# Token order of a fused attention, expert and GLU kernel: one-hot products on TensorE in the place of eighteen 4-byte scatters

## Chip, cores and metric

One core of a Trainium2 chip. The metric is the device time in microseconds of one execution of the whole program.

## What is computed

Three layers in a row over 2304 tokens of 512 features: windowed attention, a layer in which each token goes to one of eight experts, and a gated layer. The expert layer and what follows it, cut to what matters:

```python
e_idx = np.argmax(x @ w_gate, axis=1)
for e in range(8):
    mask = e_idx == e
    h = np.maximum(x[mask] @ w1[e], 0.0)
    out[mask] = gate_w[mask, None] * eom[mask, e, None] * (h @ w2[e])
x = out
g = x @ w_gate2
y = (g * (1 / (1 + np.exp(-g))) * (x @ w_val) @ w_out)
```

`y` has the tokens in their old order.

## The kernel before

**Stages.** Attention runs over 18 blocks of 128 tokens until about 160 us. As it goes, every token gets its expert (`expf`) and its rank among that expert's tokens (`rankf`), and its row is scattered to the expert's area of a DRAM buffer `xs`. Then the experts are handled in the order of their sizes, p = 0 to 7, with up to 384, 384, 352, 336, 304, 272, 256 and 256 tokens (`CAPS`). For each, `emit_xT` (L917 to L919) transposes the gathered rows on TensorE into `tx`, ScalarE copies them out as `xh` and VectorE takes the remainder `xl`; 96 matmuls of L969 make `oh` from `xh`, `xl` and the weights `w`; ScalarE makes `hh` (L977) and VectorE `hl` (L981) for each of eight chunks; 96 matmuls of L995 make `oy` from `hh`, `hl`; `oy` is stored by columns into the DRAM buffer `ys`. Last comes the gated layer over nine units of 256 columns of `ys` (L1029 to L1053); each unit's two blocks of output rows go to their places in `out` by an indirect scatter on GpSimd (L1063), whose row numbers are `oid`.

**Weights.** Every weight is loaded in 256 KB pieces by SP into one of seven staging buffers (pool `stg`): `raw` for the experts (L302), `rawd` for the gated layer (L307, 64-bit numbers that VectorE and ScalarE narrow at L281 to L286). A piece is split into a high and a low part: ScalarE makes the high one (L326, L333), VectorE the low one for experts 0 to 2 and GpSimd for the others (L328, L334). `w_step` emits these two at a time between the chunks of L969 and of L995, so on ScalarE a conversion that waits for its load holds up the `hh` behind it. From expert 1 on a load's address holds the expert's number, which is known when the experts are sorted; the first pieces of the gated layer are mixed in from the second half of expert 2's weights on.

**The order of the tokens.** `expert_tables` (VectorE, some forty small operations) sorts the experts and finds where each one's columns begin. `token_order` (L794 to L825) then finds for every token its column in `ys`: `at` (start of the expert plus rank) and `far` (for tokens beyond an expert's capacity), added to `col`, one number for each of 128 partitions and 18 blocks. Its table `scr` is a staging buffer. Eighteen indirect DMAs on GpSimd (L819) write the tokens' numbers (`toki`), 128 of 4 bytes in each, to the places `col` of a DRAM table `order`. `load_order` (L829 to L832), called at p = 2, reads the table back into `oid` as [128, 18, 1]. `overflow_tables` makes tables for tokens beyond capacity and their count `nov`, which every engine reads (L1079).

**What sets the order of the work.** Attention's order is written out by hand. Behind it a scheduler orders each engine's instructions by their data and its own estimate of times; on an engine they then run strictly in that order, and so do the DMAs of one queue.

Of the kernel before, what the change touches and what calls it, by code (L numbers as in the profile page):

```python
# [7 lines left out]
F32 = mybir.dt.float32  # L8
F32R = mybir.dt.float32r
BF16 = mybir.dt.bfloat16  # L10
I32 = mybir.dt.int32
# [15 lines left out]
def attn_moe_glu_kernel(ctx, tc, q, k, v, w_gate, w_ogate, w1, w2, w2_gate, w2_val, w2_out, out, caps=CAPS):  # L27
# [32 lines left out]
    xs = dram.tile([E * NT + 1, RW], F32, name="xs")  # L60

    ys = dram.tile([DM, NT + cap], F32, name="ys")
    order = dram.tile([NT, 1], I32, name="order")
    assert NT % 256 == 0 and caps[0] + sum(caps[1:]) >= NT and min(caps) >= 256 and CP <= 512
    NOV = (NT - min(caps) + 127) // 128
    ov_pad = dram.tile([128, NOV], I32, name="ov_pad")
# [18 lines left out]
    rankf = const.tile([128, NBLK, 1], F32, name="rankf")  # L85
    capt = const.tile([128, 1, E], F32, name="capt")
    ktab = const.tile([128, E], F32, name="ktab")
    toki = const.tile([128, NBLK], I32, name="toki")

    with ExitStack():  # L90

# [57 lines left out]
        bias = ac.tile([128, H, 128], F32, name="bias")  # L149
        tmp, tmp2 = (p_p.tile([128, 4, 128], F32, tag="p", name="tmp") for _ in range(2))  # L150
        dist, mf, mu, mt = (tmp[:, i, :] for i in range(4))
        c64, dist_i = tmp2[:, 0, :], tmp2[:, 1, :].bitcast(I32)
        mge = ac.tile([128, 128], U8, name="mge")
        m_start = ac.tile([128, 128], U8, name="m_start")
        m_mid = ac.tile([128, 128], U8, name="m_mid")
# [36 lines left out]
        it2 = ac.tile([128, 32], I32, name="it2")  # L192
        nc.gpsimd.iota(it2[:, 0:NBLK], pattern=[[128, NBLK]], base=0, channel_multiplier=1)
        nc.vector.tensor_copy(tokid, it2[:, 0:NBLK])
        nc.gpsimd.tensor_copy(toki, it2[:, 0:NBLK])
        for p in range(E):
            nc.gpsimd.memset(capt[:, 0, p:p + 1], float(caps[p]))
            nc.gpsimd.memset(ktab[:, p:p + 1], float(E - 1 - p + (1 << 15) * (p == 0)))
# [549 lines left out]
        def tb(name, shape, dt=F32):  # L748
            return tb_p.tile([128] + shape, dt, tag=name, name=name)
# [43 lines left out]

        def token_order():  # L794

            more, behind = tb("more", [1, E]), tb("behind", [1, E])
            TT(out=more, in0=cnt, in1=cape, op=ALU.subtract)
            TS(out=more, in0=more, scalar1=0.0, scalar2=None, op0=ALU.max)
            nc.vector.tensor_copy(behind, more)
            for e in range(1, E):  # L800
                TT(out=behind[:, :, e:e + 1], in0=behind[:, :, e - 1:e], in1=behind[:, :, e:e + 1], op=ALU.add)
            TT(out=behind, in0=behind, in1=more, op=ALU.subtract)
            TT(out=behind, in0=behind, in1=cape, op=ALU.subtract)
            TT(out=behind, in0=behind, in1=offe, op=ALU.subtract)
            TT(out=behind, in0=behind, in1=total.to_broadcast([128, 1, E]), op=ALU.add)
            own, pick = scratch()
            at, lim, far = (tb(nm, [NBLK, 1]) for nm in ("at", "lim18", "far"))
            full = [128, NBLK, E]
            TT(out=own, in0=iota8.unsqueeze(1).to_broadcast(full), in1=expf.to_broadcast(full), op=ALU.is_equal)
            for src, dst in ((offe, at), (cape, lim), (behind, far)):  # L810
                TT(out=pick, in0=own, in1=src.to_broadcast(full), op=ALU.mult)
                RED(out=dst, in_=pick, axis=AX, op=ALU.add)
            TT(out=at, in0=at, in1=rankf, op=ALU.add)
            TT(out=lim, in0=rankf, in1=lim, op=ALU.is_ge)
            TT(out=far, in0=far, in1=lim, op=ALU.mult)
            col = tb("col", [NBLK, 1], I32)
            TT(out=col, in0=at, in1=far, op=ALU.add)
            for j in range(NBLK):
                r = nc.gpsimd.indirect_dma_start(  # L819
                    out=order[:, :], out_offset=bass.IndirectOffsetOnAxis(ap=col[:, j, :], axis=0),  # L820
                    in_=toki[:, j:j + 1], in_offset=None,
                ).ins
                tc.declare_no_dep(r, group="order", reason="the columns of the tokens differ")
                tc.add_to_no_dep_group("order", r)
                ordered.append(r)  # L825

        ordered = []

        def load_order():  # L829
            r = nc.gpsimd.dma_start(out=oid, in_=order.rearrange("(j p) o -> p j o", p=128)).ins  # L830
            for x in ordered:
                tc.add_manual_dep(r, x.name, DATA, reason="all tokens have columns")  # L832

# [119 lines left out]
        for p in range(E):  # L955
            n = caps[p]
            xh, xl = xe.pop(p)
            if p == 0:
                token_order()
                overflow_tables()  # L960
            if p == 2:
                load_order()
            hh, hl = (grid(t, KF, n) for t in pair_tile(ht_p, "h", HW))
            for m in range(KF):
                o = ps_m.tile([128, cap], F32, tag="m", name="oh")
                i = 0
                for a, b in PASSES:
                    for kk in range(KD):
                        pace[0] = nc.tensor.matmul(  # L969
                            out=o[:, 0:n],  # L970
                            lhsT=wt["w1", p, m // 4, kk][:, a, (m % 4) * 128:(m % 4) * 128 + 128],
                            rhs=(xh, xl)[b][:, kk, :],
                            start=(i == 0),
                            stop=(i == 3 * KD - 1),
                        )
                        i += 1
                r = nc.scalar.activation(out=hh[:, m, :], in_=o[:, 0:n], func=AF.Relu).ins  # L977
                if p == 0 and m > 0:
                    with tc.issue_after(r):
                        off_reg[m] = nc.scalar.value_load(reg[0:1, 1, m:m + 1], min_val=0, max_val=NT)  # L980
                STT(out=hl[:, m, :], in0=o[:, 0:n], scalar=0.0, in1=hh[:, m, :], op0=ALU.max, op1=ALU.subtract)  # L981
                w_step(2)
                if m % 4 == 3:
                    freed[0] += 2
            if p + 1 < E:
                emit_xT(p + 1)
                load_x(p + 2)
            else:

                split_unit(0)  # L990
            o = [ps_m.tile([128, cap], F32, tag="m", name="oy") for _ in range(KD)]
            for kk in range(KF):
                for d in range(KD):
                    for i, (a, b) in enumerate(PASSES):
                        pace[0] = nc.tensor.matmul(  # L995
                            out=o[d][:, 0:n],
                            lhsT=wt["w2", p, 0, kk][:, a, d * 128:d * 128 + 128],
                            rhs=(hh, hl)[b][:, kk, :],
                            start=(kk == 0 and i == 0),
                            stop=(kk == KF - 1 and i == 2),  # L1000
                        )
                if kk % 2:
                    freed[0] += 1
                    w_step(2)

            for d in range(KD):
                y = s_p.tile([128, CP], F32, tag="sc", name="y")[:, 0:n]
                nc.scalar.activation(out=y, in_=o[d][:, 0:n], func=AF.Copy)  # L1008
                rows = ys[d * 128:d * 128 + 128, :]
                nc.scalar.dma_start(out=rows[:, 0:n] if p == 0 else rows[:, bass.ds(off_reg[p], n)], in_=y)  # L1010
            if p >= E - 2:
                load_unit(p - E + 2)
# [179 lines left out]
```

## Time and profile before

| | us |
|---|---|
| median of 3 runs | 924.95 (924.68 to 926.74) |
| the profiled execution | 926.6 |
| its span in the trace | 924.9 |
| TensorE busy | 854.8 (92%) |
| VectorE busy | 455.5 (49%) |
| ScalarE busy | 386.4 (42%) |
| GpSimd busy | 316.6 (34%) |

PE is TensorE's matmuls and PEld its loads of the stationary operand, DVE is VectorE, ACT is ScalarE, POOL is GpSimd, SP issues DMAs. A matmul's busy time includes that of the one behind it in the pipeline and grows where TensorE's clock is lowered, so a high busy share alone doesn't say that TensorE works at its best; the granted clock (PEclk, 1.00 is 2.4 GHz and 0.50 is 1.2) and the gaps are to be read beside it. The share of DMA is the mean busy share of the core's 16 DMA engines.

### The profile page before, as it was taken

The page shows a single profiled execution, that of the slowest core. Times are in us where ns is not written, and L with a number is a line of the kernel's source. Part 1 is how long each engine was busy: PE and PEld are TensorE (multiplying, and loading weights), DVE is VectorE, ACT ScalarE, POOL GpSimd, SP SyncE. Part 2 cuts the span into 40 slices and gives each one's busy share as a digit, 9 for nine tenths or more (in the row PEclk, how much of TensorE's full clock was granted, in tenths as well). Part 3 has the DMA queues.
Part 4 walks back from the last instruction along what each step waited for, and adds up shares of the span by engine and source line. Part 5 has one row for each costly group of instructions (what it writes and reads, how often), then busy time and mean ns, then how long its engine had stood idle before and what let it go on. Part 6 is the DMA issues. An engine that isn't in the chain of part 4 may idle for free.

```text
span 924.9 us, 17140 instructions
## 1 busy us (share of the span) xinstructions
PE 854.8 (92%) x6291; PEld 783.3 (85%) x6291; DVE 455.5 (49%) x1292; ACT 386.4 (42%) x1046; POOL 316.6 (34%) x388
## 2 busy tenths in 40 slices
PE   7979988689699989998988999999999999999995
PEld 5758766489599989998977989999898989899994
DVE  6777896753444563239995333324141424233240
ACT  6868873243455655656553222213121212122220
POOL 4647876143156688775563000000000000000000
PEclk9998997899899989999999999999999999999998
DMA  9996521389666677666660101010100001010000
GB/s 215 263 317 155 151 81 59 127 166 143 203 195 202 199 232 229 207 187 190 198 194 1 46 1 46 1 47 1 46 1 23 24 1 47 1 46 1 24 1 25
DMA packets 105371, 99.37 MB, mean 107 GB/s; under 512 B 62786, under 2 KB 71490, under 8 KB 105282
## 3 DMA queue, kind: packets, MB, share of 16 engines
q1 hardware_dynamic: 92752, 77.13, 31.2%
q10 hardware_dynamic: 9010, 11.59, 3.6%
q0 software_dynamic: 3520, 9.50, 2.9%
q8 instruction: 51, 0.84, 0.4%
q14 instruction: 38, 0.31, 0.1%
HBM read 77.16 MB, written 21.04 MB: 106 GB/s over the span
## 4 chain that ended last, share of the span: by engine, by line
issue 29%; PE 24%; POOL 4%; DVE 4%; DMA 2%; ACT 0%; POOLq 0%; SPq 0%; DVEq 0%; ACTq 0%
PE gv L1029 11%; PE oo L1053 7%; PE oy L995 3%; PE oh L969 3%; POOL w L328 2%; DMA rawd<-in_moe_w_val_dram 1%; DVE rawd L283 1%; DVE rawd L282 1%; POOL w L334 1%; POOL out_dram L1063 1%; DVE rawd L286 1%; DMA rawd<-in_moe_w_out_dram 0%; DMA rawd<-in_moe_w_gate_dram 0%; DMA raw<-in_moe_w_dram 0%; PE tx L917 0%
## 5 line engine op out<-in xcount | busy, mean ns | idle before, releaser
L1039 DVE TENSOR_TENSOR sg<-gv,sg 128x256 f32<-128x256 f32 x108 | 45.8, 424 | 222.3 <-ACT sg L1038 222.3
L1063 POOL DMA_INDIRECT out_dram<-xr,oid x18 | 17.4, 965 | 398.5 <-ACT xr L1062 388.7
L1053 PE MATMUL oo<-w,hh 128*128 128x512 f32 x432 | 137.7, 396 | 2.2 <-ACT w L333 1.1
L995 PE MATMUL oy<-hh,w 128*128 128x384 f32 (+5 forms) x512 | 121.1, 324 | 17.2 <-DVE hl L981 15.6
L1029 PE MATMUL gv<-xh,w 128*128 128x256 f32 x864 | 126.9, 281 | 5.2 <-DVE av L1040 5.2
L1029 PE MATMUL gv<-xh,wx 128*128 128x256 f32 x864 | 124.6, 279 | 0.0
L1029 PEld LDWEIGHTS gv<-xh,w 128*128 128x128 f32 x864 | 113.0, 189 | 6.0 <-DVE av L1040 6.0
L328 POOL TENSOR_TENSOR w<-raw,w 128x512 fp32r<-128x512 f32 x80 | 103.5, 1321 | 27.6 <-ACT w L326 14.9
L1029 PEld LDWEIGHTS gv<-xh,wx 128*128 128x128 f32 x864 | 112.0, 188 | 0.7
L995 PEld LDWEIGHTS oy<-hh,w 128*128 128x128 f32 x512 | 91.3, 199 | 20.1 <-DVE hl L981 18.2
L1053 PEld LDWEIGHTS oo<-w,hh 128*128 128x128 f32 x432 | 81.2, 188 | 22.0 <-DVE av L1040 1.5
L326 ACT ACTIVATE w<-raw 128x512 fp32r<-128x512 f32 x128 | 74.5, 623 | 53.4 <-DMA raw<-in_moe_w_dram 33.8
L969 PE MATMUL oh<-xh,w 128*128 128x384 f32 (+5 forms) x512 | 89.6, 313 | 5.1 <-ACT y L1008 5.1
L1038 ACT ACTIVATE sg<-gv 128x256 f32<-128x256 f32 x108 | 41.3, 383 | 111.9 <-PE gv L1029 96.0
L1053 PE MATMUL oo<-w,hl 128*128 128x512 f32 x216 | 85.4, 395 | 0.0
L969 PEld LDWEIGHTS oh<-xh,w 128*128 128x128 f32 x512 | 79.5, 192 | 5.7 <-ACT y L1008 5.6
L1041 ACT ACTIVATE hh<-av 128x256 fp32r<-128x256 f32 x108 | 45.2, 418 | 93.7 <-DVE av L1040 93.5
L995 PE MATMUL oy<-hl,w 128*128 128x384 f32 (+5 forms) x256 | 82.0, 321 | 0.0
L1029 PE MATMUL gv<-xl,w 128*128 128x256 f32 x432 | 68.9, 281 | 0.0
L1029 PE MATMUL gv<-xl,wx 128*128 128x256 f32 x432 | 68.1, 279 | 0.0
L1043 DVE TENSOR_TENSOR hl<-av,hh 128x256 fp32r<-128x256 f32 x98 | 41.6, 425 | 44.4 <-ACT hh L1041 44.4
L1062 ACT ACTIVATE xr<-oo 128x512 f32<-128x512 f32 x18 | 10.8, 599 | 120.0 <-PE oo L1053 119.3
(203 smaller groups left out, 1487.2 us busy)
## 6 DMA issues: line engine op xcount, KB each, us to landing
raw<-in_moe_w_dram SPq DMA_DIRECT2D x128, 256.0 KB
xs<-zrow ACTq DMA_DIRECT2D x8, 774.0 KB
rawd<-in_moe_w_gate_dram SPq DMA_DIRECT2D x24, 256.0 KB
rawd<-in_moe_w_val_dram SPq DMA_DIRECT2D x24, 256.0 KB
rawd<-in_moe_w_out_dram SPq DMA_DIRECT2D x24, 256.0 KB
xr<-xs SPq DMA_DIRECT2D x6, 774.0 KB
xr<-ys SPq DMA_DIRECT2D x9, 512.0 KB
qr<-in_q_dram SPq DMA_DIRECT2D x16, 256.0 KB
```

Source lines behind the costliest of these rows:

```text
L326: nc.scalar.activation(out=s[:, 0, :], in_=t, func=AF.Copy)
L328: low = lambda: eng.tensor_tensor(out=s[:, 1, :], in0=t, in1=s[:, 0, :], op=ALU.subtract)
L969: pace[0] = nc.tensor.matmul(out=o[:, 0:n], lhsT=wt["w1", p, m // 4, kk][:, a, (m % 4) * 128:(m % 4) * 128 + 128], rhs=(xh, xl)[b][:, kk, ...
L995: pace[0] = nc.tensor.matmul(out=o[d][:, 0:n], lhsT=wt["w2", p, 0, kk][:, a, d * 128:d * 128 + 128], rhs=(hh, hl)[b][:, kk, :], start=(kk ...
L1029: nc.tensor.matmul(out=gv[:, i, :], lhsT=wt[nm, -1, m // 4, kk][:, a, (m % 4) * 128:(m % 4) * 128 + 128], rhs=(xh, xl)[b][:, kk, :], start ...
L1038: nc.scalar.activation(out=sg, in_=gv[:, 0, :], func=AF.Sigmoid)
L1039: TT(out=sg, in0=gv[:, 0, :], in1=sg, op=ALU.mult)
L1041: nc.scalar.activation(out=ah[:, m, :], in_=av, func=AF.Copy)
L1043: (nc.gpsimd if u == 0 and m < 10 else nc.vector).tensor_tensor(out=al[:, m, :], in0=av, in1=ah[:, m, :], op=ALU.subtract)
L1053: nc.tensor.matmul(out=o[c], lhsT=(ah, al)[b][:, kk, c * 128:c * 128 + 128], rhs=wt["o", -1, 0, kk][:, a, :], start=(kk == 0 and i == 0), ...
L1062: nc.scalar.activation(out=ob[:, c, :], in_=o[c], func=AF.Copy)
L1063: r = nc.gpsimd.indirect_dma_start(out=out[:, :], out_offset=bass.IndirectOffsetOnAxis(ap=oid[:, 2 * u + c, :], axis=0), in_=ob[:, c, :], ...
```

## The change

The scatters, the table `order`, its load and `toki` go. With `col` known, VectorE splits it into a high part (`at`, column divided by 128) and a low part (`far`, the rest). For block j, `here` is a table of 128 x 128 that holds a one where the column's low part is c, and `what` a table of 18 columns with the partition's number, and 18 with the block's number, in the column of the high part, zero elsewhere. The product of `here` and `what`, summed over the eighteen blocks in PSUM, gives for every column the partition and the block of its token, and 128 times the block plus the partition is `oid`. `which` and `here` use the pool `s_p` (two buffers, tag `sc`), `what` a staging buffer.

```diff
-    order = dram.tile([NT, 1], I32, name="order")
...
-    toki = const.tile([128, NBLK], I32, name="toki")
+    iota128 = const.tile([128, 128], BF16, name="iota128")
+    jblk = const.tile([128, 1, NBLK], F32, name="jblk")
...
-        nc.gpsimd.tensor_copy(toki, it2[:, 0:NBLK])
+        nc.gpsimd.iota(it_i[:, 0:NBLK], pattern=[[1, NBLK]], base=0, channel_multiplier=0)
+        nc.vector.tensor_copy(jblk[:, 0, :], it_i[:, 0:NBLK])
+        nc.gpsimd.iota(col_i, pattern=[[1, 128]], base=0, channel_multiplier=0)
+        nc.vector.tensor_copy(iota128, col_i)
...
             TT(out=col, in0=at, in1=far, op=ALU.add)
-            for j in range(NBLK):
-                r = nc.gpsimd.indirect_dma_start(
-                    out=order[:, :], out_offset=bass.IndirectOffsetOnAxis(ap=col[:, j, :], axis=0),
-                    in_=toki[:, j:j + 1], in_offset=None,
-                ).ins
...
-        def load_order():
-            r = nc.gpsimd.dma_start(out=oid, in_=order.rearrange("(j p) o -> p j o", p=128)).ins
...
+            ca, cb_ = tb("ca", [NBLK, 1], I32), tb("cb", [NBLK, 1], I32)
+            TS(out=ca, in0=col, scalar1=7, scalar2=None, op0=ALU.logical_shift_right)
+            TS(out=cb_, in0=col, scalar1=127, scalar2=None, op0=ALU.bitwise_and)
+            nc.vector.tensor_copy(at, ca)
+            nc.vector.tensor_copy(far, cb_)
+            sq = [128, NBLK, NBLK]
...
+            TT(out=which, in0=jblk.to_broadcast(sq), in1=at.to_broadcast(sq), op=ALU.is_equal)
+            TS(out=what[:, :, 0, :], in0=which, scalar1=tokid[:, 0:1], scalar2=None, op0=ALU.mult)
+            TT(out=what[:, :, 1, :], in0=which, in1=jblk.rearrange("p a j -> p j a").to_broadcast(sq), op=ALU.mult)
+            o = ps_m.tile([128, 2, NBLK], F32, tag="m", name="oid_ps")
+            NB_ = CP * 2 // 128
+            for j0 in range(0, NBLK, NB_):
+                here = s_p.tile([128, CP], F32, tag="sc", name="here").bitcast(BF16).rearrange("p (j c) -> p j c", c=128)
+                for j in range(j0, min(j0 + NB_, NBLK)):
+                    TS(out=here[:, j - j0, :], in0=iota128, scalar1=far[:, j, :], scalar2=None, op0=ALU.is_equal)
+                    nc.tensor.matmul(
+                        out=o, lhsT=here[:, j - j0, :], rhs=what[:, j], start=(j == 0), stop=(j == NBLK - 1)
+                    )
+            nc.vector.tensor_copy(at[:, :, 0], o[:, 0, :])
+            STT(out=oid[:, :, 0], in0=o[:, 1, :], scalar=128.0, in1=at[:, :, 0], op0=ALU.mult, op1=ALU.add)
...
-            if p == 2:
-                load_order()
```

The scheduler puts the new instructions at these places. First TensorE, from the transposes of expert 0 on, in the program before:

```order
L917 MATMUL tx<-ident,xr 128x128 x12
L969 MATMUL oh<-xh,w 128x384 x16
L969 MATMUL oh<-xl,w 128x384
L969 MATMUL oh<-xh,w 128x384
L969 MATMUL oh<-xl,w 128x384
```

and in the changed program, whose lines stand 13 (L917) and 11 (L969) further down; of the six pairs of a load and a product that stand between the transposes and L980 the last two are shown:

```order
L841 LDWEIGHTS here
L841 MATMUL oid_ps<-what,here 128x36
L841 LDWEIGHTS here
L841 MATMUL oid_ps<-what,here 128x36
L980 MATMUL oh<-xh,w 128x384 x4
L980 MATMUL oh<-xl,w 128x384 x4
L980 MATMUL oh<-xh,w 128x384 x8
L980 MATMUL oh<-xl,w 128x384 x2
L841 LDWEIGHTS here
L841 MATMUL oid_ps<-what,here 128x36
```

Six of the new products stand between the transposes of expert 0 and its first product; the other twelve stand behind 18 of those.

Then VectorE at the end of `token_order`, before, where `far` and `col` are made among weight conversions (L328), the tables of the overflow (L857 to L860) and the first `hl`:

```order
L328 TENSOR_TENSOR w<-raw,w 128x512
L812 TENSOR_REDUCE far<-scr 128x18
L857 TENSOR_REDUCE ib<-scr 128x16
L328 TENSOR_TENSOR w<-raw,w 128x512
L815 TENSOR_TENSOR far<-far,lim_2769 128x18
L328 TENSOR_TENSOR w<-raw,w 128x512
L858 TENSOR_TENSOR ib<-bf,ib 128x16
L860 TENSOR_TENSOR scr<-scr,omore 128x128
L981 SCALAR_TENSOR_TENSOR hl<-oh,hh 128x384
L817 TENSOR_TENSOR col<-at,far 128x18
```

and in the changed program, from the last step of `far` on:

```order
L821 TENSOR_TENSOR col<-at,far 128x18
L823 TENSOR_SCALAR ca<-col 128x18
L824 TENSOR_SCALAR cb<-col 128x18
L825 CAST at<-ca 128x18
L826 CAST far<-cb 128x18
L832 TENSOR_TENSOR which<-jblk,at 128x324
L840 TENSOR_SCALAR here<-iota_81,far 128x128 x6
L833 TENSOR_SCALAR what<-which,tokid 128x18x18
L834 TENSOR_TENSOR what<-which,jblk 128x18x18
L860 TENSOR_TENSOR scr<-omore,lim 128x128
L840 TENSOR_SCALAR here<-iota_81,far 128x128 x12
L861 TENSOR_REDUCE nb<-scr 128x8
```

The whole chain to the tables now stands in one piece behind the four `xl` of expert 0, and the first weight conversion and most of the overflow's tables stand behind it.

## Rows read from the trace of the kernel before

**Rows 1.** Windows: stretch, length; PE, PEld, DVE, ACT, POOL busy (count); clock, DMA share, GB/s

```profile
179.76:196.92 17.16, 17.16 (x100) 17.13 (x99) 13.85 (x52) 9.45 (x19) 4.92 (x5) 0.98 0.85 228
197.98:222.71 24.73, 19.00 (x100) 18.37 (x99) 9.40 (x22) 7.00 (x14) 13.06 (x13) 0.93 0.91 141
222.54:246.35 23.81, 19.82 (x99) 19.47 (x99) 7.40 (x16) 8.78 (x19) 2.79 (x3) 0.86 0.75 145
249.19:272.31 23.12, 20.00 (x98) 19.17 (x99) 11.85 (x24) 11.45 (x26) 10.88 (x10) 0.85 0.63 193
...
288.74:308.06 19.32, 17.41 (x101) 17.12 (x100) 11.10 (x18) 10.55 (x24) 15.56 (x14) 0.91 0.73 218
...
324.00:345.14 21.14, 18.10 (x101) 17.82 (x99) 12.77 (x20) 10.80 (x26) 17.65 (x16) 0.84 0.74 225
```

**Rows 2.** Timeline of TensorE: start and length in us, [idle before, and its releaser]

```profile
177.31 2.79 PE L917 MATMUL tx<-ident,xr 128*128 128x128 f32 x12 [9.21 <-DVE nb L848]
...
193.98 1.55 PE L969 MATMUL oh<-xh,w 128*128 128x384 f32 x8
195.36 0.86 PE L969 MATMUL oh<-xl,w 128*128 128x384 f32 x4
...
196.76 1.47 PE L917 MATMUL tx<-ident,xr 128*128 128x128 f32 x12
```

**Rows 3.** Timeline of TensorE, its gaps in experts 0 and 1

```profile
203.74 0.45 PE L995 MATMUL oy<-hh,w 128*128 128x384 f32 x1 [1.52 <-DVE w L328]
...
209.96 0.44 PE L995 MATMUL oy<-hh,w 128*128 128x384 f32 x1 [4.20 <-DVE hl L981]
...
239.18 1.65 PE L969 MATMUL oh<-xh,w 128*128 128x384 f32 x4 [3.99 <-ACT y L1008]
```

**Rows 4.** Timeline of ScalarE, a conversion that waits for its load

```profile
201.87 0.63 ACT L326 ACTIVATE w<-raw 128x512 fp32r<-128x512 f32 x1 [5.91 <-DMA raw<-in_moe_w_dram]
```

**Rows 5.** DMA queues from 195 to 235 us, and below from 250 to 300 us

```profile
DMA packets 3632, 5.41 MB, mean 135 GB/s; under 512 B 986, under 2 KB 1097, under 8 KB 3630
...
q1 hardware_dynamic: 2821, 5.19, 87.6%
...
q0 software_dynamic: 546, 0.01, 1.8%
...
DMA packets 5681, 10.26 MB, mean 205 GB/s; under 512 B 575, under 2 KB 1087, under 8 KB 5675
```

**Rows 6.** Instructions on the table order: count, ns min/median/max, first and last start

```profile
L819 POOL DMA_INDIRECT order<-toki,col x18: 957/962/1762, 190.8 to 220.2; - x18
L830 POOL DMA_DIRECT2D oid<-order x1: 1291/1291/1291, 233.9 to 233.9; - x1
```

**Rows 7.** Timeline of VectorE, at the start and from 172 us

```profile
4.41 1.16 DVE L173 TENSOR_SCALAR bias<-tmp 128x128 f32<-128x128 f32 x8
...
8.94 0.69 DVE L391 COPY_PREDICATED s<-mge,s 128x512 f32<-128x512 uint8 x1 [2.29 <-PE s L365]
...
172.34 0.30 DVE L809 TENSOR_TENSOR scr<-iota,expf 128x144 f32<-128x144 f32 x1
...
172.94 1.32 DVE L782 TENSOR_TENSOR end<-end,held 128x1 f32<-128x1 f32 x7
...
180.67 0.56 DVE L919 TENSOR_TENSOR xl<-tx,xh 128x384 fp32r<-128x384 f32 x1
...
187.28 0.69 DVE L328 TENSOR_TENSOR w<-raw,w 128x512 fp32r<-128x512 f32 x1 [3.27 <-ACT w L326]
```

**Rows 8.** Timeline of TensorE, six small products

```profile
161.31 0.29 PE L765 MATMUL cnt_ps<-gs,ones 128*128 128x8 bf16 x6
```

**Rows 9.** Windows from 420 us, then two pieces of the chain that ended last

```profile
420.00:440.00 20.00, 16.65 (x134) 15.75 (x133) 20.00 (x46) 12.76 (x37) 10.63 (x14) 1.00 0.66 195
...
386.12 0.93 PE oy L995 x8
...
388.30 2.54 POOL w L328 x2
```

More of the change, by code (lines that the diff above doesn't have):

```diff
@@ L151, in attn_moe_glu_kernel @@
         dist, mf, mu, mt = (tmp[:, i, :] for i in range(4))
-        c64, dist_i = tmp2[:, 0, :], tmp2[:, 1, :].bitcast(I32)
+        c64, dist_i, col_i = tmp2[:, 0, :], tmp2[:, 1, :].bitcast(I32), tmp2[:, 2, :].bitcast(I32)
         mge = ac.tile([128, 128], U8, name="mge")
@@ L817, in token_order @@
             TT(out=col, in0=at, in1=far, op=ALU.add)
-            for j in range(NBLK):
-                r = nc.gpsimd.indirect_dma_start(
-                    out=order[:, :], out_offset=bass.IndirectOffsetOnAxis(ap=col[:, j, :], axis=0),
-                    in_=toki[:, j:j + 1], in_offset=None,
-                ).ins
-                tc.declare_no_dep(r, group="order", reason="the columns of the tokens differ")
-                tc.add_to_no_dep_group("order", r)
-                ordered.append(r)
@@ L827, in attn_moe_glu_kernel @@
-        ordered = []
-        def load_order():
-            r = nc.gpsimd.dma_start(out=oid, in_=order.rearrange("(j p) o -> p j o", p=128)).ins
-            for x in ordered:
-                tc.add_manual_dep(r, x.name, DATA, reason="all tokens have columns")
+            ca, cb_ = tb("ca", [NBLK, 1], I32), tb("cb", [NBLK, 1], I32)
+            TS(out=ca, in0=col, scalar1=7, scalar2=None, op0=ALU.logical_shift_right)
+            TS(out=cb_, in0=col, scalar1=127, scalar2=None, op0=ALU.bitwise_and)
@@ new lines, in token_order @@
+            nc.vector.tensor_copy(at, ca)
+            nc.vector.tensor_copy(far, cb_)
+            sq = [128, NBLK, NBLK]
+            which = s_p.tile([128, CP], F32, tag="sc", name="which")[:, 0:NBLK * NBLK].rearrange(
+                "p (j a) -> p j a", a=NBLK)
+            what = stg.tile([128, 512], F32, tag="stg", name="what").bitcast(BF16)[:, 0:2 * NBLK * NBLK].rearrange(
+                "p (j i a) -> p j i a", i=2, a=NBLK)
+            TT(out=which, in0=jblk.to_broadcast(sq), in1=at.to_broadcast(sq), op=ALU.is_equal)
```

## Prediction, made before the changed kernel ran

> **What bounds the kernel now.** I read the stages first, then the gaps of TensorE in them, then whom the waiting engines wait for, and the DMA engines last. In [rows 1] each stretch is one stage of the tensor engine: the products of L969 and of L995 for expert 0, the same two for expert 1, then the second stage of experts 2 and 3. Every stage of experts 0 and 1 is 96 products of 384 columns. What they cost unhindered is in [rows 2]: eight products start at 193.98 and the next at 195.36, 0.173 us each, so 96 take 16.6 us. Against that the second stage of expert 0 (24.73 us) is 8.1 us too long, the first of expert 1 (23.81) 7.2, its second (23.12) 6.5, and the turn between the two (246.35 to 249.19 in [rows 1], 2.8 us against 1.1 us from 196.92 to 197.98) 1.8. That is 23.6 us lost between 198 and 272 us, as gaps [rows 3] and as half clock behind the gaps (the granted clock of these stages is 0.85 to 0.93).
>
> The gaps name VectorE or ScalarE, but those only pass a wait on. In [rows 4] ScalarE's conversion of a weight (L326) waits 5.91 us for the DMA of its raw tile, and the activation hh that TensorE needs stands behind it in program order. The weights are late because the DMA engines are full without moving much. From 195 to 235 us they moved 135 GB/s; from 250 to 300 us, with the same kinds of loads, 205 GB/s [rows 5]. What runs in the first stretch and not in the second are the eighteen 4-byte scatters (L819, 190.8 to 220.2 us) and the element-wise load of the table behind them (L830, 233.9) [rows 6]. The scatters' own packets hold the engines for only 1.8% of that time [rows 5], so their harm, if it is theirs, is that other packets stand behind them: the queue of the weights was charged 87.6% for 5.19 MB.
>
> Beside [rows 5] stands a rule that speaks against this reading: the Trainium skill, DMA: Bandwidth & Descriptors, section SWDGE vs HWDGE vs iDMA, says that DMAs issued from GpSimd and from SP feed different internal queues of each DMA engine, and that the engine takes turns between them. By that rule packets of 1.8% could hardly hold back the others; the trace does not agree so far, as the weights' queue slows in that very stretch. The rule is followed out as the second rival.
>
> **The change, part by part.** *Removed:* eighteen scatters (0.96 us of GpSimd each) and one table load [rows 6]. GpSimd's own time is free, since nobody waits for GpSimd there. What counts is the DMA traffic. If it is the cause, the 23.6 us shrink to what an expert of the same mix of loads loses without scatters. The second stages of experts 2 and 3 [rows 1] tell that: 352 and 336 columns should take 15.2 and 14.6 us and took 19.3 and 21.1, so 4.1 and 6.6 us are lost; the wide weights that they load begin in expert 1's time. I leave 5.4 us for expert 1 and nothing for expert 0. Gain 23.6 - 5.4 = 18.2 us. The bounds are 0 (the scatters are not the cause) and 23.6.
>
> *Added on the path:* six of the eighteen new products stand on TensorE ahead of the first product of L969, and twelve more after 18 of those. TensorE has finished its transposes at 180.1 (177.31 + 2.79, [rows 2]) and began L969 at 179.8. Now it waits for VectorE to have `col`, six tables `here` and both halves of `what`. VectorE is through with xl at 181.2 (180.67 + 0.56, [rows 7]). From there, in the order shown above:
> - eight steps of `behind`, each needing the one before, at 0.19 us (seven in 1.32 us, [rows 7]): 1.5 us;
> - a product and a reduction over 144 columns at 0.30: 0.6; `far` and `col`: 0.4; four conversions, two of them dependent: 0.6;
> - `which`, 324 columns: between 0.30 (144 columns) and 0.69 (512): 0.45; the two halves of `what`, as wide: 0.9;
> - six `here` at 0.145 us (eight one-input operations of 128x128 in 1.16 us, [rows 7]): 0.9.
>
> That is 5.35 us, to 186.6. Six small products of the kind of [rows 8] (six in 0.29 us at full clock) make 0.6 at half clock, and L969 begins at 187.2 instead of 179.8: 7.4 us. TensorE will have stood for 6.5 us, and the row of the transposes behind the 9.21 us gap shows what follows: 2.79 us where the same twelve take 1.47 later [rows 2]. I put 1.7 us for half clock at the restart (1.3, that row, to 3.4, a stage at 0.85 clock), and 0.5 for the other twelve products. **Added: 9.5 us.** Low bound 8, with `here` and `what` cheaper; high bound 13, with each `here` at 0.29, each 324-column operation at 0.69 and the longer slow clock.
>
> *Moved:* The tables of the overflow come later on VectorE, behind the order. `nov` is then made behind three hl, near 195 us, and SP's load of `nov` moves from behind five weight loads to behind fourteen; the fifteenth load stands behind it. That load needs a staging buffer which the eighth conversion frees at about the same time, so I put nothing; at worst it is 2 us late and lands in conversions that TensorE needs only for expert 1, 20 us on. The conversions' second halves (L328) start later on VectorE by the 18 `here`, 2.6 us; expert 1's weights are not needed before 220, so nothing. ScalarE issues its two small overflow stores earlier: nothing. `what` holds one of the seven staging buffers until the last small product: nothing, by the same reserve. At the start two iotas and two casts come in: VectorE stood 2.29 us idle before 8.94 [rows 7], which covers them; without that cover they cost 0.4. The output scatters (L1063) read `oid` only at 509 us: nothing.
>
> **The sum.** 18.2 - 9.5 = 8.7 us less by the end of expert 1. It has to be carried to the end. From 272 on the order of every engine is the same in both programs, and each load waits for a buffer that TensorE's progress frees, so I take the later stages as moved as a whole. Speaking against it is the stretch from 420 to 440 us, where VectorE is busy 20.00 of 20 us [rows 9], largely with narrowing the wide weights: that bound moves only if its loads come earlier too. They do if the chain behind it does; it passes from TensorE to GpSimd between 387 and 388 us [rows 9], so it hangs on TensorE's progress. The profiled execution took 926.6 us (span 924.9) and gives 917.9; the median of the runs, 924.95, is 1.65 us lower, and so I say **916.3 us**. For this case alone: 911 to 922, from the bounds of 8 and 13 us added and 2 to 8 us left over in expert 1.
>
> **Rivals.**
> - *Nothing is left over* in expert 1, and the later waits shrink too. For: the gap at 239 us [rows 3] may be an echo of loads issued before 235. Against: experts 2 and 3 lose 4 to 7 us with no scatter near. 23.6 - 9.5 = 14 us or somewhat more: 908 to 911.
> - *The scatters are not what starves the weights.* Then the loads come as late as now, 0 us are gained, and TensorE's new stop before L969 is all that is left: up to 9.5 us, 934 us; part of it covers waits that come anyway (5.7 us of gaps before 210 us, [rows 3]), so 928 to 934. Place: the first product of L969. It decides for slower as soon as less than 9.5 of the 23.6 us come back. For: the scatters' packets take 1.8%. Against: the stretch of 135 GB/s begins and ends with them. The rule on separate queues cited above would make this the outcome.
> - *The gain is made and lost again.* The weights of experts 2 to 7 come no earlier, because conversion on GpSimd and VectorE is what paces them, and TensorE waits there instead. For: VectorE's 20.00 of 20. Against: the chain that ends last runs through TensorE until 387 us [rows 9], so up to there the weights were in time. 0 to 5 us are kept: 920 to 925.
>
> **Numbers.** A measurement of this kernel can tell about 0.2% (1.9 us) from no change. Forecast 0.58, nothing left over 0.15, lost again 0.12, scatters innocent 0.15. Of the third, half lies within 1.9 us of the old time. So faster 0.79, same 0.07, slower 0.14. The range runs from 908, the far end of the first rival, to 927, which takes in the lost gain and leaves out most of the slower case: about 0.16 lie outside.
>
> **What would show it.** Right: a gap of 6 to 7 us on TensorE between the transposes and L969 near 180 to 187 us; over 180 GB/s from 195 to 235 us; ScalarE's waits for raw weights under 3 us each; the second stage of expert 0 near 17 us and expert 2 begun near 263 instead of 272. Wrong: 135 GB/s again in that stretch, a gap over 9 us, or a TensorE that starts expert 2 earlier and reaches 490 us at the old time.

## The result, and the profile after

The changed kernel takes 909.38 us (median, 908.81 to 910.95) where the kernel before, on the same chip, takes 924.82: a ratio of 0.9834, with a 95% interval from 0.9813 to 0.9855. In a later series of runs the same pair gave 0.9796 (0.9782 to 0.9810), so ratios from different series are to be compared to some 0.4% only. The profiled execution took 909.5 us, its span in the trace is 907.7 us, against 924.9 before. The forecast was 916.3 in a range of 908 to 927: the direction held, and the gain of 15.4 us is nearly twice the 8.7 us forecast.

The windows of the changed kernel, with the columns of [rows 1]. The first stretch is TensorE's stop, the second the first products of expert 0; then the second stage of expert 0, both stages of expert 1, and the second stages of experts 2 and 3:

```profile
179.76:186.50 6.74, 0.38 (x3) 0.11 (x2) 6.25 (x30) 1.74 (x4) 0.00 (x0) 0.50 0.76 252
186.49:205.29 18.80, 18.80 (x116) 18.61 (x116) 17.24 (x63) 9.33 (x19) 0.00 (x0) 0.92 0.64 208
206.36:223.25 16.89, 16.89 (x100) 16.89 (x99) 8.24 (x15) 7.52 (x16) 0.00 (x0) 1.00 0.64 204
223.09:239.89 16.80, 16.80 (x99) 16.76 (x99) 10.87 (x24) 9.63 (x22) 2.04 (x3) 1.00 0.58 178
240.96:257.84 16.88, 16.88 (x101) 16.88 (x99) 8.36 (x17) 9.22 (x20) 9.46 (x9) 1.00 0.70 229
274.27:293.60 19.33, 17.42 (x101) 17.13 (x100) 11.08 (x18) 10.65 (x24) 15.55 (x14) 0.91 0.73 217
309.53:330.49 20.96, 18.09 (x101) 17.82 (x100) 12.73 (x20) 10.86 (x26) 17.68 (x16) 0.84 0.73 232
```

Read them against [rows 1]. Rows three to five have come from 24.73, 23.81 and 23.12 us down to 16.8 and 16.9 each: PE's busy time now equals the length of the stretch, and the granted clock is 1.00 (2.4 GHz). The last two rows stand as before (19.32 and 21.14 us). The first row is new: TensorE does nothing for 6.4 us and is then granted half its clock (the first four products of L980 take 1.42 us, from 186.67 to 188.09, where four take 0.69 in expert 1).

The timeline of TensorE in the changed kernel shows the new stop, the turn between the stages of expert 0 at 205.13, the start of expert 2, and the two old stops of over 1 us that are left in experts 2 and 3 (columns as in [rows 2]):

```profile
177.34 2.80 PE L930 MATMUL tx<-ident,xr 128*128 128x128 f32 x12 [7.23 <-DMA xr<-xs]
186.49 0.34 PE L841 MATMUL oid_ps<-what,here 128*128 128x36 bf16 x6 [6.36 <-DVE what L834]
186.67 1.63 PE L980 MATMUL oh<-xh,w 128*128 128x384 f32 x4
188.09 1.48 PE L980 MATMUL oh<-xl,w 128*128 128x384 f32 x4
...
205.13 1.47 PE L930 MATMUL tx<-ident,xr 128*128 128x128 f32 x12
206.36 0.42 PE L1006 MATMUL oy<-hh,w 128*128 128x384 f32 x1
...
257.68 0.81 PE L980 MATMUL oh<-xh,w 128*128 128x352 f32 x4
...
277.39 0.43 PE L1006 MATMUL oy<-hh,w 128*128 128x352 f32 x1 [1.91 <-DVE hl L992]
...
316.51 0.65 PE L1006 MATMUL oy<-hh,w 128*128 128x336 f32 x1 [2.87 <-DVE hl L992]
```

None of the gaps of [rows 3] is there any more. The stop is VectorE's chain, whose last steps are, in VectorE's timeline of the changed kernel:

```profile
184.26 0.50 DVE L832 TENSOR_TENSOR which<-jblk,at 128x324 f32<-128x324 f32 x1
184.68 1.06 DVE L840 TENSOR_SCALAR here<-iota,far 128x128 bf16<-128x128 bf16 x6
185.65 0.39 DVE L833 TENSOR_SCALAR what<-which,tokid 128x324 bf16<-128x324 f32 x1
185.95 0.49 DVE L834 TENSOR_TENSOR what<-which,jblk 128x324 bf16<-128x324 f32 x1
```

And the DMA queues of the changed kernel between 195 and 235 us, the stretch of [rows 5]:

```profile
DMA packets 4669, 8.08 MB, mean 202 GB/s; under 512 B 620, under 2 KB 1132, under 8 KB 4666
...
q1 hardware_dynamic: 3944, 7.25, 58.0%
```

Half as much again is moved as before (202 GB/s against 135), while the weights' queue q1 is charged less of the engines' time (58.0% against 87.6% for 5.19 MB). ScalarE's waits for raw weights are shorter too. Only the first of them is over 3 us, and it stands in the trace of before as well (5.98 us, at 186.61):

```profile
185.52 3.29 ACT L329 ACTIVATE w<-raw 128x512 fp32r<-128x512 f32 x5 [4.86 <-DMA raw<-in_moe_w_dram]
...
194.88 0.63 ACT L329 ACTIVATE w<-raw 128x512 fp32r<-128x512 f32 x1 [1.40 <-DMA raw<-in_moe_w_dram]
```

Up to the end of expert 1 none of the later ones is over 1.9 us, where [rows 4] shows one of 5.91.

### The profile page after: what moved, and what is told of

It reads as the page before. It is cut to its first block, busy times and chain, and to the rows that moved or that the text cites. A ratio compares the mean times of both kernels' runs of the same rounds, so it can differ in the third digit from the quotient of the medians.

```text
span 907.7 us, 17184 instructions
## 1 busy us (share of the span) xinstructions
PE 847.5 (93%) x6309; PEld 777.8 (86%) x6309; DVE 457.0 (50%) x1321; ACT 386.6 (43%) x1046; POOL 296.1 (33%) x370
## 4 chain that ended last, share of the span: by engine, by line
issue 35%; PE 22%; DVE 4%; POOL 2%; DMA 2%; ACT 1%; POOLq 0%; DVEq 0%; ACTq 0%
PE gv L1040 8%; PE oo L1064 6%; PE oy L1006 4%; PE oh L980 3%; DVE rawd L285 2%; DVE rawd L286 2%; POOL out_dram L1074 1%; DMA rawd<-in_moe_w_val_dram 1%; DVE rawd L289 1%; POOL w L337 1%; DMA rawd<-in_moe_w_out_dram 0%; DMA rawd<-in_moe_w_gate_dram 0%; PE tx L930 0%; ACT rawd L284 0%; ACT w L329 0%
## 5 line engine op out<-in xcount | busy, mean ns | idle before, releaser
L1006 PE MATMUL oy<-hh,w 128*128 128x384 f32 (+5 forms) x512 | 117.3, 317 | 7.0 <-DVE hl L992 6.9
L331 POOL TENSOR_TENSOR w<-raw,w 128x512 fp32r<-128x512 f32 x80 | 103.4, 1319 | 26.7 <-ACT w L329 13.5
L1006 PEld LDWEIGHTS oy<-hh,w 128*128 128x128 f32 x512 | 88.8, 194 | 8.2 <-DVE hl L992 8.2
L980 PE MATMUL oh<-xh,w 128*128 128x384 f32 (+5 forms) x512 | 87.3, 310 | 1.0 <-ACT y L1019 1.0
L980 PEld LDWEIGHTS oh<-xh,w 128*128 128x128 f32 x512 | 78.3, 189 | 1.3 <-ACT y L1019 1.2
```

The costliest lines, as they stand in the source:

```text
L331: low = lambda: eng.tensor_tensor(out=s[:, 1, :], in0=t, in1=s[:, 0, :], op=ALU.subtract)
L980: pace[0] = nc.tensor.matmul(out=o[:, 0:n], lhsT=wt["w1", p, m // 4, kk][:, a, (m % 4) * 128:(m % 4) * 128 + 128], rhs=(xh, xl)[b][:, kk, ...
L1006: pace[0] = nc.tensor.matmul(out=o[d][:, 0:n], lhsT=wt["w2", p, 0, kk][:, a, d * 128:d * 128 + 128], rhs=(hh, hl)[b][:, kk, :], start=(kk ...
```

## The experiments

Theory A is the prediction's: the eighteen 4-byte scatters starve the loads of the weights, and the stop before expert 0 is what the change pays for their removal. Its rivals: the load of the table does it, or the scatters are innocent and something else of the change does it. (The letters in the quoted expectations are given anew in each.) Each run is given as its ratio to the kernel before, on the same chip.

The expectations name times of the first two traces. In the later series the kernel before took 919.1 to 923.4 us, and in their traces expert 0 begins earlier: its transposes start at 170.8 to 174.2 us instead of 177.3. So I compare times by ratio, and places by one distance on TensorE, from the start of expert 0's transposes to the first product of expert 2. It is 94.8 us in the kernel before (177.31 to 272.14) and 80.3 in the changed kernel (177.34 to 257.68), 80.7 in a second trace of it (e0_after).

### The scatters back, unread (e1_scatters_back)

```diff
+            for j in range(18):
+                r = nc.gpsimd.indirect_dma_start(
+                    out=order[:, :], out_offset=bass.IndirectOffsetOnAxis(ap=col[:, j, :], axis=0),
+                    in_=toki[:, j:j + 1], in_offset=None,
+                ).ins
             ca, cb_ = tb("ca", [NBLK, 1], I32), tb("cb", [NBLK, 1], I32)
```

> The changed kernel with the eighteen 4-byte scatters into a table put back behind col; nobody reads the table, and the order still comes from the products. Theory A (the scatters hold up the weights' packets): the stretch from 195 to 235 us falls from 202 GB/s to 130 to 160, single conversions on ScalarE wait 5 us or more for raw weights, expert 2 starts at 268 to 278 us instead of 257.7, and the time is 922 to 932 us. Theory B (the scatters were innocent, and the loads are in time because the new order of the engines or the later start of expert 0 lets them be): 909 to 912 us, with over 190 GB/s in that stretch.

Measured: 917.99 us, ratio 0.9989 (0.9974 to 1.0004): by the ratio the whole gain is given back, though the order still comes from the products and nobody waits for these scatters. The windows of this run at the turn between the stages of expert 0 and in its second stage:

```profile
198.83:205.83 7.00, 2.05 (x13) 1.41 (x11) 2.33 (x7) 1.75 (x4) 3.79 (x4) 0.84 0.98 71
207.59:227.64 20.05, 19.91 (x97) 19.40 (x98) 11.68 (x29) 9.05 (x17) 0.00 (x0) 0.84 0.96 230
```

In the turn the DMA engines are 98% busy and move 71 GB/s. TensorE's timeline there:

```profile
198.83 1.15 PE L940 MATMUL tx<-ident,xr 128*128 128x128 f32 x9
204.93 0.90 PE L940 MATMUL tx<-ident,xr 128*128 128x128 f32 x3 [4.95 <-DVE hl L1002]
207.59 0.69 PE L1016 MATMUL oy<-hh,w 128*128 128x384 f32 x1 [1.76 <-DVE hl L1002]
```

These stops are of the kind of [rows 3], though not at the same products: the scatters now run from 178 to 206 us, 13 us earlier than in [rows 6], and the harm ends with them, as both stages of expert 1 take 16.8 to 16.9 us. From the transposes to the first product of the second stage it is 8.8 us (198.83 to 207.59) where the changed kernel has 1.2 (205.13 to 206.36), and the stage behind takes 20.0 us instead of 16.9: 7.5 + 3.2 = 10.7 us. The distance to expert 2 agrees with it: 91.0 us, 10.3 to 10.6 more than in the changed kernel and 3.9 less than before. So the harm is smaller than theory A put it: 176 GB/s between 195 and 235 us, and expert 2 begun at 262.1 us. The ratios say 14 to 18 us (0.9989 against 0.9834 or 0.9796); this profiled execution, at 915.2 us, is the fastest of ten and 2.8 us under their median, and where what is still missing goes is not shown.

### The scatters left out of the kernel before (e4_no_order)

The scatters and the load go and `oid` gets the tokens' own numbers: no order is computed, and the output rows go to wrong places.

```diff
-            for j in range(NBLK):
-                r = nc.gpsimd.indirect_dma_start(
...
+            nc.vector.tensor_copy(oid[:, :, 0], toki)
...
-            if p == 2:
-                load_order()
```

> The kernel before with the scatters and the load of the table left out and nothing in their place: oid is a copy of the tokens' numbers as they stand, so the order of the output rows is not computed. It prices the removal alone. Theory A: the 23.6 us lost in experts 0 and 1 go and nothing is added: 900 to 904 us, and expert 2 starts near 249 us. Theory B: 922 to 925 us.

Measured: 896.67 us, ratio 0.9761 (0.9732 to 0.9789). Its windows for the second stage of expert 0 and both stages of expert 1:

```profile
192.34:209.23 16.89, 16.89 (x100) 16.89 (x99) 10.63 (x25) 8.02 (x16) 0.00 (x0) 1.00 0.83 277
209.06:225.87 16.81, 16.81 (x99) 16.77 (x99) 10.53 (x24) 9.38 (x22) 1.60 (x3) 1.00 0.55 177
226.94:243.82 16.88, 16.88 (x101) 16.88 (x100) 8.34 (x16) 8.88 (x20) 9.14 (x9) 1.00 0.70 230
```

Hardly anything is left over in these three stages. Removal alone is worth 2.39%, 22.1 of 924.8 us, close to the upper bound of 23.6; the distance to expert 2 is 72.2 us, 22.6 less than before. What the change adds costs 0.4 to 0.7% by the two ratios of the changed kernel, which are of other series, and 8.2 to 8.5 us by that distance.

### Scatters or load (e9_no_load, e10_load_back)

Once the kernel before without the load (the scatters run, nobody reads their table, and `oid` again holds no order), once the changed kernel with an element-wise load of such a table alone:

```diff
+            nc.vector.tensor_copy(oid[:, :, 0], toki)
             for j in range(NBLK):
                 r = nc.gpsimd.indirect_dma_start(
...
-            if p == 2:
-                load_order()
```

```diff
+            if p == 1:
+                r = nc.gpsimd.dma_start(out=oid2, in_=order.rearrange("(j p) o -> p j o", p=128)).ins
+                tc.add_manual_dep(r, pace[0].ins.name, DATA, reason="behind expert 0")
```

> The kernel before without the element-wise load of the table (L830); the eighteen scatters stay, and oid is a copy of the tokens' numbers as they stand, so the order of the output rows is not used. With the scatters put back the changed kernel lost only 10 of the 23.6 us in experts 0 and 1, and nothing in expert 1. Theory A (the load, 2304 descriptors of 4 bytes at 234 us, makes the loss in expert 1): 8 to 13 us less than before, ratio 0.986 to 0.992. Theory B (the scatters alone make both, and expert 1's loss is the echo of expert 0's): less than 2 us, ratio 0.998 to 1.000.

> The changed kernel with an element-wise load of a 4-byte table put back alone, behind expert 0's last product; the table is filled by one plain store during attention, and nobody reads what is loaded. Theory A (the load costs by itself what expert 1 lost): a gap of 3 us or more on TensorE in expert 1, and 6 to 12 us more than the changed kernel, ratio to the kernel before 0.990 to 0.997. Theory B (the load is harmless without the scatters): within 2 us of the changed kernel, ratio 0.982 to 0.986.

Measured: 922.37 us, ratio 1.0002 (0.9983 to 1.0022), without the load; 908.39 us, ratio 0.9859 (0.9827 to 0.9891), with the load alone. TensorE's timeline of the first has the stops of [rows 3]:

```profile
205.01 0.69 PE L994 MATMUL oy<-hh,w 128*128 128x384 f32 x1 [6.24 <-DVE hl L980]
...
237.25 1.65 PE L968 MATMUL oh<-xh,w 128*128 128x384 f32 x4 [5.22 <-ACT y L1007]
```

The load falls as a cause from both sides. Without it nothing is gained. With it alone the ratio is 0.3 to 0.6% above the changed kernel's in the other series, hardly more than those two differ by; the traces decide it, for the distance to expert 2 is 80.6 us, as in the changed kernel (80.3 and 80.7). The gain is the scatters'.

### What about them is dear (e2_wide_scatters, e8_rows64, e13_words_apart)

The run with the scatters put back, each time with one thing changed: rows of 512 bytes, rows of 64 bytes, and 4-byte words again, but each 512 bytes from the next.

```diff
-    order = dram.tile([NT, 1], I32, name="order")
+    order = dram.tile([NT, 128], I32, name="order")
...
-                    in_=toki[:, j:j + 1], in_offset=None,
+                    in_=toki[:, :], in_offset=None,
```

```diff
-    order = dram.tile([NT, 1], I32, name="order")
+    order = dram.tile([NT, 16], I32, name="order")
...
-                    in_=toki[:, j:j + 1], in_offset=None,
+                    in_=toki[:, :], in_offset=None,
```

```diff
-    order = dram.tile([NT, 1], I32, name="order")
+    order = dram.tile([NT * 128, 1], I32, name="order")
...
+            TS(out=cw, in0=col, scalar1=7, scalar2=None, op0=ALU.logical_shift_left)
...
-                    out=order[:, :], out_offset=bass.IndirectOffsetOnAxis(ap=col[:, j, :], axis=0),
+                    out=order[:, :], out_offset=bass.IndirectOffsetOnAxis(ap=cw[:, j, :], axis=0),
```

> As the run with the scatters put back, but each of the 128 rows of a scatter has 512 bytes instead of 4 (zeros into a wider table that nobody reads): 1.18 MB in place of 9 KB, the same number of descriptors. If the harm lies in the number of descriptors that GpSimd's queue hands the DMA engines, the time is that of the run with 4 bytes or up to 5 us above it. If it lies in the writes being so small, it falls back to 909 to 915 us, the 1.18 MB being worth some 5 us of the DMA engines at 205 to 230 GB/s.

> The changed kernel with eighteen scatters put back whose rows have 64 bytes (zeros into a table that nobody reads). With 4 bytes the ratio to the kernel before was 0.999, with 512 bytes 0.986. If the price lies in any write far below 512 bytes, it is that of 4 bytes, 0.995 to 1.000. If it lies in writes of single words, it is that of 512 bytes, 0.983 to 0.987. Between the two it falls with the size.

> The changed kernel with the eighteen 4-byte scatters put back, but each word 512 bytes from the next in a table 128 times as long. Theory W (a 4-byte write is dear by itself): the second stage of expert 0 takes 19 to 21 us again, 170 to 180 GB/s between 195 and 235 us, and a ratio of 0.995 to 1.000 as with the scatters side by side. Theory N (dear is that many writes fall into the same few lines of DRAM at once): stages of 16.8 to 17.0 us, 195 to 205 GB/s, and a ratio of 0.983 to 0.987 as with rows of 64 and 512 bytes.

| scatters in the changed kernel | us | ratio (interval) | distance to expert 2, us | issue to landing, median us | GB/s, 185 to 200 us |
|---|---|---|---|---|---|
| 4 bytes, side by side (e1) | 917.99 | 0.9989 (0.9974 to 1.0004) | 91.0 | 12.9 | 108 |
| 4 bytes, 512 apart (e13) | 908.40 | 0.9845 (0.9823 to 0.9867) | 80.5 | 3.8 | 237 |
| 64 bytes (e8) | 909.35 | 0.9874 (0.9837 to 0.9910) | 80.5 | 3.6 | 233 |
| 512 bytes (e2) | 906.12 | 0.9859 (0.9837 to 0.9881) | 80.7 | 4.0 | 262 |

The scatters run from 178 to 206 us in the first and from 179 to 203 in the others, so 185 to 200 lies inside all of them. The DMA queues in that stretch, of the run with the words side by side:

```profile
DMA packets 1115, 1.62 MB, mean 108 GB/s; under 512 B 330, under 2 KB 330, under 8 KB 1114
...
q1 hardware_dynamic: 878, 1.61, 81.2%
q0 software_dynamic: 236, 0.00, 3.3%
```

and of the run with the same words 512 bytes apart:

```profile
DMA packets 2252, 3.55 MB, mean 237 GB/s; under 512 B 528, under 2 KB 528, under 8 KB 2250
...
q1 hardware_dynamic: 1930, 3.53, 73.2%
q0 software_dynamic: 320, 0.01, 1.5%
```

The same instructions with the same 4 bytes for each token: more of the scatters' packets pass (320 against 236), and beside them the weights' queue moves 3.53 MB instead of 1.61. In the page's list of DMA issues one scatter takes 12.9 us to land in the first run and 3.8 in the second:

```profile
order<-toki,col POOLq DMA_INDIRECT x18, 12.9
```

```profile
order<-toki,cw POOLq DMA_INDIRECT x18, 3.8
```

So neither the number of scatters nor the size of a write is dear by itself. Dear is that the words lie side by side: 2304 of them in 9 KB of DRAM. The other three kinds run beside expert 0's work as well, and up to expert 2 they cost nothing that the traces show (80.5 to 80.7 us, as in the changed kernel). Over the whole kernel the words set apart are 3.0 us slower than the changed kernel in the same series (908.40 against 905.42, 0.9845 against 0.9796); in the traces that difference lies behind expert 1, where the second stages of experts 2 and 3 differ by 1 to 2 us between the two traces of the changed kernel itself. Whether the scatters cost it is not shown. After the runs with 64 and 512 bytes alone I had taken the smallness for the cause (theory W in the last expectation); that falls. What the memory does with such writes no run shows, nor from which distance on they are harmless: single words were tried side by side and 512 bytes apart alone, rows that begin 64 bytes apart only with all 64 bytes written. The kernel before with its own words set apart, and so without the products, wasn't tried.

### The products elsewhere (e3_late, e11_later)

Once `token_order` is called at the turn to the fifth expert (p = 4); once its VectorE part stays, and the products are emitted behind chunks 4, 5 and 6 of expert 0's first stage:

```diff
             if p == 0:
-                token_order()
                 overflow_tables()
+            if p == 4:
+                token_order()
```

```diff
-                token_order()
+                products = token_order()
...
+                if p == 0 and m in (4, 5, 6):
+                    products((4, 5, 6).index(m) * (CP * 2 // 128))
```

> The changed kernel with token_order() called at expert 4 instead of expert 0, so that the products stand behind expert 3's on TensorE and VectorE's tables are made among later work. Theory A (the stop of TensorE before L980 costs what it measured, expert 0's first stage ending at 205.3 instead of 196.9 us, and later stages move as a whole): 8 us less, 900 to 903 us, with no gap over 1 us between the transposes and L980. Rival: conversions of weights pace experts 2 to 7 anyway, and TensorE waits there for what it gained: 906 to 910 us.

> The changed kernel with its tables made where they are, but the products emitted in three groups behind chunks 4, 5 and 6 of expert 0's first stage, so that TensorE finds the tables ready. Theory A (the stop before the first product is the whole price of the new order, 8.4 us between the ends of expert 0's first stage in the two traces, of which 0.8 us are the products themselves): no gap between the transposes and L992, 7 to 8 us less than the changed kernel, ratio to the kernel before 0.975 to 0.978. Rival (the gap moves behind chunk 4, or to the next wait, as it did when the whole order was put at expert 4): 0.981 to 0.985.

The first: 910.29 us, ratio 0.9907 (0.9882 to 0.9932), slower than the changed kernel, so theory A missed. The early stop is gone (73.4 us to expert 2), but TensorE's timeline shows a longer one at the later turn. The scheduler set the products ahead of the first L981 of that expert and VectorE came to `what` late:

```profile
327.27 0.24 PE L841 MATMUL oid_ps<-what,here 128*128 128x36 bf16 x2 [9.14 <-DVE what L834]
327.38 1.35 PE L981 MATMUL oh<-xh,w 128*128 128x304 f32 x4
```

The second: 898.74 us, ratio 0.9736 (0.9709 to 0.9763), a little under theory A's. The products now slip in between the matmuls of the first stage without a wait:

```profile
185.11 0.32 PE L851 MATMUL oid_ps<-what,here 128*128 128x36 bf16 x6
...
187.45 0.32 PE L851 MATMUL oid_ps<-what,here 128*128 128x36 bf16 x6
...
191.17 0.22 PE L851 MATMUL oid_ps<-what,here 128*128 128x36 bf16 x2
```

That is the ratio of the kernel that finds no order at all (0.9761), within the two intervals. The distance to expert 2 is 73.1 us, 72.2 without any order and 80.3 to 80.7 in the changed kernel: nearly all that the change pays is TensorE's stop with the slow clock behind it, and some 0.9 us stay. The gain over the changed kernel is between 0.6 and 1.0%, by its two ratios.

### What is left in experts 2 and 3 (e0_after, e5_low_dve, e12_later_low)

The prediction left 5.4 us over in expert 1 because experts 2 and 3 lose 4 to 7 us with no scatter near. Expert 1 loses nothing, so I asked what those two lose it to. In the traces GpSimd makes the low parts of the weights of expert 3 (L331) at 1.3 us a piece, where VectorE takes 0.69 [rows 7]; I took the loads to wait for the staging buffers that these conversions set free. The edit gives expert 3's low parts to VectorE; the last run adds it to the products later on. The changed kernel itself ran beside them.

```diff
-                        eng = nc.gpsimd if name[1] >= 3 else nc.vector
+                        eng = nc.gpsimd if name[1] >= 4 else nc.vector
```

> The changed kernel itself, beside the three others on one chip. Every theory: 0.9813 to 0.9855 of the kernel before, as measured, and the same stages in the profile (first experts' stages of 16.8 to 16.9 us, one stop of about 6.4 us ahead of the six products).

> The changed kernel with the low parts of expert 3's weights taken by VectorE, as those of experts 0 to 2 are, instead of GpSimd. Theory R (what is lost in expert 2's second stage, 19.3 us against 16.9 us, comes from GpSimd's conversions of 1.3 us, which set the staging buffers free too late for the loads): that stage comes down to 17 to 17.5 us and the time falls by 2 to 4 us, ratio to the kernel before 0.979 to 0.982. Theory S (that stage is held by the loads' bandwidth alone, whichever engine converts): the stage stays at 18.5 to 19.5 us, and the ratio at 0.983 to 0.985. If VectorE becomes the later one there: a stage over 19.5 us and a ratio over 0.985.

> The products behind chunks 4 to 6 of expert 0's first stage, as before, and expert 3's low parts on VectorE. Theory R: the gains add, ratio 0.969 to 0.972. Theory S: as the products later alone, 0.973 to 0.975. The stage of expert 2 as in the run with the low parts alone.

Measured, all on one chip: the changed kernel 905.42 us, ratio 0.9796 (0.9782 to 0.9810); with VectorE 902.00, 0.9763 (0.9746 to 0.9780); with the products later too 893.77, 0.9673 (0.9659 to 0.9686). The second stages of experts 2 and 3 in the three runs' windows, first the changed kernel:

```profile
271.50:288.79 17.29, 15.86 (x101) 15.57 (x100) 9.90 (x18) 10.42 (x24) 13.51 (x13) 1.00 0.72 222
306.25:326.05 19.80, 16.87 (x98) 16.59 (x99) 12.38 (x19) 9.22 (x23) 16.36 (x15) 0.91 0.76 232
```

then with the low parts on VectorE:

```profile
268.82:288.96 20.14, 17.68 (x101) 17.10 (x100) 14.75 (x25) 11.68 (x26) 9.95 (x10) 0.92 0.63 201
304.90:321.17 16.27, 15.34 (x101) 15.06 (x100) 10.93 (x17) 8.57 (x22) 13.65 (x13) 1.00 0.81 258
```

and with both edits:

```profile
264.02:280.68 16.66, 16.15 (x101) 15.57 (x100) 13.14 (x22) 10.71 (x25) 9.28 (x9) 1.00 0.71 220
297.08:314.20 17.12, 15.59 (x98) 15.04 (x99) 10.88 (x19) 10.01 (x25) 13.89 (x14) 1.00 0.74 241
```

All three ratios lie 0.2 to 0.3% under the expected ones, the changed kernel's own too. With VectorE the time fell by 3.4 us, within the 2 to 4 that theory R gave, but not where it said: expert 2's stage did not come down to 17 us (it took 20.1), expert 3's did (16.3). Nor is expert 2's loss the same from run to run: the changed kernel itself took 19.33 us there in the first trace and 17.29 in this one. Expert 3's stage took 19.5 to 21.4 us in every trace of this study with its low parts on GpSimd, and 16.3 and 17.1 in the two with them on VectorE. So the conversions on GpSimd are most of what held expert 3 (the prediction's measure for its 336 columns is 14.6 us). What holds expert 2, and why it took 16.7 us with both edits, stays open. The last kernel is the fastest of the study, 3.3% below the kernel before and 1.3% below the changed one on the same chip.

## Why the prediction was right, and where it was off

- **The bound and its cause: right, and shown.** Scatters out: 2.4% gained, and the three stages behind expert 0's first at 16.8 to 16.9 us. Scatters back: by the ratio nothing gained, in the trace 10.3 to 10.6 us given back. The load has no part in it. Which scatters are dear the prediction didn't ask: words side by side are, words set apart and wider rows did not delay expert 2.
- **The range held, the forecast's own bounds did not.** For its own case the prediction gave 911 to 922 us, and 909.4 lies below. It lies in the stated range because that was drawn out to 908 for the rival "nothing is left over", which had a chance of 0.15 and came true in experts 0 and 1. The hit is in part luck.
- **The gain: right in kind, 4.6 us too small.** From the end of expert 0's first stage to the end of expert 1 it took 272.31 - 196.92 = 75.4 us before and 257.84 - 205.29 = 52.6 after: 22.8 us, where the sum had 18.2 out of 23.6 lost. The step that failed is "I leave 5.4 us for expert 1": measured with the same 16.6 us for a stage, 0.8 is left in experts 0 and 1 together, and no gap. The yardstick was experts 2 and 3, whose loss has causes of its own (for expert 3, as the last runs show, conversions on GpSimd). The stop of 3.99 us at 239 us [rows 3] went with the scatters, as the rival "nothing is left over" had it; its 908 to 911 us is where the time lies.
- **The added part: right, 1.1 us too large.** The first stage of expert 0 ends at 205.29 instead of 196.92, 8.4 us later against 9.5 (the terms 7.4, 1.7 and 0.5 add to 9.6). VectorE's chain ended at 186.44 (forecast 186.6). The six small products took 0.2 us until the first L980 at 186.67, not 0.6, because L980 starts in the pipeline behind them; half clock and the other twelve products made that stage 18.6 us for 17.2, 1.5 us instead of 2.2. The sizes that were bounded came out at 0.50 for `which` (0.45 taken), 0.39 and 0.49 for the halves of `what` (0.45 each), and 0.18 for one `here` (0.145).
- **The moved steps: nothing, as taken.** From expert 0's second stage to the end of expert 1 no stage is longer than 16.9 us, so neither the later load of `nov`, nor the later conversions, nor the staging buffer lent to `what` shows in it.
- **Carried to the end: right.** Expert 2's first products start at 257.68 instead of 272.14, 14.5 us earlier; experts 2 and 3 have the stages they had; the spans differ by 17.2, the medians by 15.4. So some 2.7 us more come behind that point in these two traces; no run shows why. The rival in which the gain is lost again falls.
- **The scatters innocent: falls, with the rule beside it in this case.** The Trainium skill, DMA: Bandwidth & Descriptors, section SWDGE vs HWDGE vs iDMA, says that DMAs issued from GpSimd and from SP feed different queues in each DMA engine, and that the engine takes turns between these. The runs agree with it for 64-byte rows, for 512-byte rows and for words set apart (80.5 to 80.7 us to expert 2 with all eighteen scatters running, as without them); with the words side by side the weights' queue halves (1.61 MB against 3.53), whatever turns are taken. The Trainium skill, DMA: Bandwidth & Descriptors, section Specifications, says that below 512 bytes a DMA engine reads, modifies and writes; by that alone I would expect the 64-byte rows and the words apart to be dear too, and they are not (80.5 us each, against 91.0 with the words side by side).

## What to carry to other kernels

When loads are late, set the bytes moved beside the busy share of the DMA engines: much busy time for few bytes points to what else runs in that stretch, however small its own share (1.8% here). A scatter of single words into a packed DRAM table can cost a neighbouring load stream half its rate; before replacing it by arithmetic, try the words 512 bytes apart, or rows of 64 bytes; in this kernel neither delayed expert 2, though neither was tried in the kernel before. A product that hangs on a long chain of VectorE belongs between the tensor engine's later matmuls, not ahead of the next stage: here that brought the price of the order from some 8 us down to 1.

## What the runs showed of the hardware that I had not expected

- 128-word scatters of 4 bytes land in 12.9 us (median) when their words lie side by side and in 3.8 us when they lie 512 bytes apart, and beside them all queues together move 108 and 237 GB/s (185 to 200 us).
- Rows of 512 bytes, 128 times the data, cost no more than words set apart: ratios 0.9859 and 0.9845, whose intervals overlap, and 80.7 and 80.5 us to expert 2.
- A load of single 4-byte elements from such a packed table did no harm (80.6 us to expert 2, 80.3 and 80.7 without it), though the scatters into one did.
